# 29 small loads of different shapes between two weight loads at the end of a decode kernel

## Chip, core and metric

The kernel runs on one core of one Trainium2 chip. The metric is the device time of one execution in microseconds (us). The kernel before takes 1329.65 us (median of 3 runs, 1329.64 to 1329.71).

## What is computed

One decode step for a batch of two rows of 1024 numbers. A gate `g`, from the row and a weight vector, mixes two branches: `a` is multi-head attention over a cache, `b` a small MLP with two residual layers. Cut to what matters:

```python
B, Sq, D, H, Sk, Dh, F = 2, 1, 1024, 32, 16384, 128, 3584

def _A_ref(x, k_cache, v_cache, wq, wo):            # caches: (B, H, Sk, Dh), bf16
    q = (x @ wq).reshape(B, Sq, H, Dh).transpose(0, 2, 1, 3)
    scores = jnp.einsum("bhqd,bhkd->bhqk", q, k_cache) * (Dh ** -0.5)
    p = softmax(scores, axis=-1)
    o = jnp.einsum("bhqk,bhkd->bhqd", p, v_cache)
    return o.transpose(0, 2, 1, 3).reshape(B, Sq, H * Dh) @ wo

def _B_ref(x, w1, w2, w3, w4):
    h = gelu(layernorm(x) @ w1)
    hs = shifted(h) @ w2                            # parts of h moved along the sequence, which has length 1
    x1 = x + hs
    return x1 + gelu(layernorm(x1) @ w3) @ w4

g = sigmoid((x * gate_w).sum(-1, keepdims=True))
return g * a + (1 - g) * b
```

The caches are 2 x 32 x 16384 x 128 numbers of two bytes each for K and for V, 537 MB together. The rest, weights and inputs, is some 36 MB.

## The kernel before

**Tiles.** One large SBUF tile, `mem`, is cut into five cells of 16,384 numbers (32 KB) per partition; `region(cell, elements, offset)` names a part of it. A K or V block (two heads of one batch row, 128 partitions x 32,768 numbers, 8.4 MB, one transfer) fills two neighbouring cells: K goes to cells 0 and 1 for the first batch row and to 1 and 2 for the second (`K_CELL`), V to 3 and 4 (`V_CELL`), and the last V block to 0 and 1 (`V_LAST`).

**Loops.** Heads go in pairs (`HP` = 16 pairs, two batch rows each, so 32 units). A unit loads K, turns it in 128 x 2048 blocks on VectorE (line 435), forms the scores by matmuls on TensorE (line 441), takes the softmax (`softmax_a`, `softmax_b`), loads V and multiplies by it (`pv`, line 495), and scales the result (`pv_end`). `tc.For_i` runs over the pairs with `odd_unit` and `even_unit`; in the last round a `tc.If` block runs `last_unit`. The MLP's first layers run ahead of the loop.

**Order of transfers.** All large loads are issued by SyncE, from one queue and in program order (`load_k` line 113, `load_v` line 118, `load_weight` line 91); only w2 and the output go through ScalarE. `in_order()` ties each engine's instructions to the order of the program, so a transfer written between two others is issued between them. A load that would overwrite a cell waits at SyncE until the cell's readers are done, and all later issues wait behind it.

**The tail.** `last_unit` loads what the output needs, as listed in `TAIL`: piece 0 is wo (8.4 MB), 1 to 3 are w4 in 16, 9 and 3 of its 28 rows per partition, 4 to 6 the five rows of w1 that were left out at the start. Every row of a piece is 2 KB on each of 128 partitions. `load_tail(k)` (line 567) issues a piece and gives it a semaphore of its own, counted up by 16. Pieces 0 and 1 go to cells 3, 4 and 2 and are issued after `pv(0)`; the others go to cells 0 and 1, over the last V block, and stand after `pv(1, V_LAST)`. In `output()` TensorE waits for each piece in turn and runs its matmuls (`add_rows`, line 402): wo with the turned heads, w4 with `h2T`, then the rest of w1. `write_out()` runs after the last piece of w4 and stores the two rows; after the last piece of w1 a last gelu runs on ScalarE (line 663). At the very end GpSimd waits until the store has landed.

These lines of `output()` set the order in which the pieces are awaited:

```python
for k, (group, cell, at, src, r, n) in enumerate(TAIL):
    nc.tensor.wait_ge(tail_sems[k], 16)
```

Of the kernel before, what the change touches and what calls it, by code (L numbers as in the profile page):

```python
# [11 lines left out]
BF16 = mybir.dt.bfloat16  # L12
# [11 lines left out]
def kernel(  # L24
# [15 lines left out]
    nc = tc.nc  # L40
    P = nc.NUM_PARTITIONS
# [24 lines left out]
    const = ctx.enter_context(tc.tile_pool(name="const", bufs=1))  # L66
# [33 lines left out]
    rows = const.tile([B + 1, D], BF16, name="rows")  # L100
# [16 lines left out]
    def load_v(hp, b, cell=V_CELL):  # L117
        nc.sync.dma_start(out=region(cell, NJ * Dh), in_=cache_rows(A_v_cache, hp, b))
# [6 lines left out]
        out=ident_s[:], in0=ident_f[:], scalar1=-scale, scalar2=None, op0=ALU.mult  # L125
# [10 lines left out]
        out=mask4[:], in_=mask4[:], compare_op=ALU.is_ge, fill=0.0,  # L136
# [3 lines left out]
        out=mask4[:], in_=mask4[:], compare_op=ALU.is_ge, fill=0.0,  # L140
# [11 lines left out]
        out=lmat[:].rearrange("p (g h k) -> p g h k", h=2, k=4),  # L152
        in_=hm2[:].unsqueeze(1).unsqueeze(3).to_broadcast([P, P // 8, 2, 4]),
# [5 lines left out]
        out=lane[:],  # L159
        in_=ident_f[:].rearrange("p (c k) -> p k c", k=QP),  # L160
# [5 lines left out]
    for g in range(Q4):  # L166
        nc.vector.tensor_scalar(
            out=spread[:, g],
# [159 lines left out]
    for shift in (1, -1, 2, -2):  # L328
# [10 lines left out]
        out=x1_rows[:], in_=oacc[1][:, 0:G1], func=ACTF.Copy, scale=omg_row[:, 0:1]  # L339
# [21 lines left out]
    for k in range(2):  # L361
        wide = mlp.tile([P, 16, QP], FP32, tag="wide", name="wide")
        nc.scalar.activation(  # L363
            out=wide[:].rearrange("p (c e) i -> p c e i", e=2),
            in_=oacc[k][:].rearrange("p (c i e) -> p c e i", i=QP, e=2),
# [15 lines left out]
    for e in range(2):  # L381
        half = slice(e * HALF, (e + 1) * HALF)
        nc.vector.tensor_copy(
            out=qdu[half].rearrange("p u v -> p (u v)"),
            in_=qdps[half, e].rearrange("p k g n -> p (k g n)"),
# [27 lines left out]
    def begin_rows(into, saved):  # L413
        for g in range(Q4):
            nc.tensor.matmul(
                into[g][QP * g : QP * g + B, 0:G1],
                lhsT=ident_f[:, QP * g : QP * g + B],
                rhs=saved[:],
                start=True,
                stop=False,  # L420
                skip_group_check=True,
            )
# [29 lines left out]
    def score_first(hp, b):  # L452
        write_qw(hp, b)
        score_chunks(b, halves[1 - b], True, False)

    def score_second(b):
        score_chunks(b, halves[b], False, True)

    def softmax_a(b):
        S = S_tiles[b]  # L460
        st = ppool.tile([P, GT, QP], FP32, name="St")
        nc.vector.transpose(out=st[:].rearrange("p j r -> p (j r)"), in_=S[:])  # L462
        m = stat.tile([P, 1], FP32, name="m")
        nc.vector.tensor_reduce(out=m[:], in_=st[:, :, 0:NG], axis=AX.XY, op=ALU.max)  # L464
        Dm = ppool.tile([P, P], FP32, name="Dm")
        nc.scalar.activation(out=Dm[:], in_=ident_s[:], func=ACTF.Copy, scale=m[:, 0:1])  # L466
        st_tiles[b] = (st, Dm)

    def softmax_b(b):
        st, Dm = st_tiles.pop(b)  # L470
        R_ps = misc_psum([P, P])
        nc.tensor.matmul(R_ps[:], lhsT=ones_f[:], rhs=Dm[:], start=True, stop=True)  # L472
        nb = stat.tile([P, 1], FP32, name="nb")
        rs = stat.tile([P, 1], FP32, name="rs")
        parts = [slice(e * HALF, (e + 1) * HALF) for e in range(2)]
        for rows in parts:
            nc.vector.tensor_reduce(out=nb[rows], in_=R_ps[rows, rows], axis=AX.X, op=ALU.min)  # L477
        for e, rows in enumerate(parts):
            nc.scalar.activation(  # L479
                out=pts[b][rows, :, e, :].rearrange("p (m a) k -> p a k m", a=GT // 4),  # L480
                in_=st[rows, :, 0:NG].rearrange("p (a k) m -> p a k m", k=4),
                func=ACTF.Exp,
                bias=nb[rows],
                scale=scale,
                accum_out=rs[rows],
            )
        tot_ps = misc_psum([P, 1])
        nc.tensor.matmul(tot_ps[:], lhsT=lmat[:], rhs=rs[:], start=True, stop=True)  # L488
        nc.vector.reciprocal(out=rinvs[b][:], in_=tot_ps[:])  # L489

    def pv(b, cell=V_CELL):
        V = view(cell)
        for g in range(NJ // 4):
            q = g % Q4
            nc.tensor.matmul(  # L495
                oacc[b][QP * q : QP * q + 8, :],
                lhsT=pts[b][:, g].rearrange("p h k -> p (h k)"),
                rhs=V[:, 4 * g : 4 * g + 4, :].rearrange("p j d -> p (j d)"),
                start=(g < Q4),
                stop=(g >= NJ // 4 - Q4),  # L500
            )
# [4 lines left out]
    def pv_end(hp, b):  # L506
        osb = ppool.tile([P, 4 * Dh], FP32, name="osb")
        nc.scalar.activation(  # L508
            out=osb[:], in_=oacc[b][:], func=ACTF.Copy, scale=rinvs[b][:, 0:1]
        )  # L510
        ot = misc_psum([P, 2])
        for k in range(4):
            nc.tensor.matmul(  # L513
                ot[:], lhsT=osb[:, k * Dh : (k + 1) * Dh], rhs=lane[:, k : k + 5 : 4],
                start=(k == 0), stop=(k == 3),
            )
        nc.vector.tensor_scalar(  # L517
            out=o_all[:, b, bass.ds(2 * hp, 2)], in0=ot[:], scalar1=g_rep[:, b : b + 1],
            scalar2=None, op0=ALU.mult,
        )  # L520
# [5 lines left out]
    def turn_heads():  # L526
        apart = mlp.tile([P, B, H, Q4], BF16, name="apart")
        for b in range(B):
            nc.vector.tensor_tensor(
                out=apart[:, b],  # L530
                in0=o_all[:, b].unsqueeze(2).to_broadcast([P, H, Q4]),
                in1=mask4[:].unsqueeze(1).to_broadcast([P, H, Q4]),
                op=ALU.mult,
            )
        ps = misc_psum([P, B, QP])
        for b in range(B):
            nc.tensor.matmul(
                ps[:, b], lhsT=apart[:, b].rearrange("p h c -> p (h c)"), rhs=lane_b[:],
                start=True, stop=True,
            )  # L540
        t = mlp.tile([P, QP, B], BF16, name="o_turned")
        nc.vector.tensor_copy(out=t[:], in_=ps[:].rearrange("p b r -> p r b"))
        return t
# [17 lines left out]
    def tail_piece(k):  # L561
        group, cell, at, src, r, n = TAIL[k]
        return region(cell, n * D, at * D)

    def load_tail(k):
        group, cell, at, src, r, n = TAIL[k]
        dma = nc.sync.dma_start(out=tail_piece(k), in_=src[:, r * D : (r + n) * D])
        dma.then_inc(tail_sems[k], 16)
        tc.no_tile_sem_insts.add(dma.ins.name)
        tc.add_to_no_dep_group(group, dma.ins)  # L570


    end_mark = const.tile([1, 1], FP32, name="end_mark")
    stored = tc.alloc_semaphore("stored")
    out_row = mlp.tile([B, D], BF16, name="out_row")
# [51 lines left out]
    def last_unit(hp):  # L627
        V_LAST = 0
        score_first(hp, 1)
        load_v(hp, 1, V_LAST)  # L630
        score_second(1)
        softmax_a(1)
        pv(0)
        load_tail(0)
        load_tail(1)
        pv_end(hp, 0)
        softmax_b(1)
        pv(1, V_LAST)
        for k in range(2, len(TAIL)):
            load_tail(k)  # L640
        pv_end(hp, 1)

    def output():
        begin_rows(arows, x1_rows)
        o_turned = turn_heads()
        hidden = [oacc[0]] * Q4
        begin_rows(hidden, h_early)
        nc.scalar.activation(
            out=h_rows[0:1, 0:1], in_=o_turned[0:1, 0, 0:1], func=ACTF.Gelu_apprx_tanh
        )  # L650
        for k, (group, cell, at, src, r, n) in enumerate(TAIL):
            nc.tensor.wait_ge(tail_sems[k], 16)
            if src is wo_rows:
                add_rows(arows, o_turned, 0, tail_piece(k), False, group)
            elif src is w4_rows:
                mm = add_rows(arows, h2T, r, tail_piece(k), r + n == FC, group)
                if r + n == FC:
                    tc.declare_fence(mm.ins, group=group)
                    write_out()
            else:  # L660
                mm = add_rows(hidden, xn1T, r, tail_piece(k), r + n == KC, group)
                tc.declare_fence(mm.ins, group=group)
        nc.scalar.activation(out=h_rows[:], in_=oacc[0][:, 0:G1], func=ACTF.Gelu_apprx_tanh)  # L663
        mark = nc.gpsimd.memset(end_mark[:], 0.0)
        tc.declare_fence(mark.ins, group="stored")
        nc.gpsimd.wait_ge(stored, 16)

    def in_order():

# [59 lines left out]
```

## Time and profile before

| what | value |
|---|---|
| median of 3 runs | 1329.65 us |
| the profiled execution | 1329.7 us |
| its span, first to last instruction | 1327.7 us |
| TensorE clock granted, mean over the span | 0.782 |
| busy share: TensorE / VectorE / ScalarE / GpSimd | 57% / 49% / 10% / 1% |
| read from HBM | 572.53 MB, 431 GB/s over the span |
| SyncE: wo issued / its first matmul | 1272.94 / 1305.93 us |
| SyncE: last five pieces issued | 1288.85 to 1291.95 us |
| last instruction that computes (ScalarE, line 663) | ends 1326.87 us |

The engines are PE (TensorE matmul), PEld (TensorE weight load), DVE (VectorE), ACT (ScalarE), POOL (GpSimd) and SP (SyncE); a q behind the name (SPq) means the engine's sequencer, which issues transfers. L567 is line 567 of the kernel. The page gives the busy share of 40 equal slices of the span in tenths, with the transfer engines in the row DMA (mean over the core's 16 transfer engines). A transfer is cut into packets; a packet is what one transfer engine moves at a time. A row of a timeline has the start in us, the time from first to last of the merged instructions in us, engine, line, operation, tile and count, and in brackets the idle time before it with what ended it. A row of the stages has the stage, its length, the busy time (and count) of PE, PEld, DVE, ACT and POOL, the granted clock, the share of the transfer engines that was busy, and GB/s.

### The profile page before, as it was taken

The numbers are of one execution on the slowest core, as the hardware profiler recorded it, in microseconds if no ns is written. First come the engines' busy times: TensorE is split into PE (matmuls) and PEld (weight loads), VectorE is DVE, ScalarE is ACT, GpSimd is POOL, SyncE is SP. The second block draws the span as 40 slices with busy tenths as digits, with TensorE's granted clock in tenths as the row PEclk, the third lists the DMA queues.
The fourth block names the chain that finished last, engine by engine and source line by source line (L and its number), as shares of the span: only waits on it lengthen the run. The fifth ranks groups of instructions, "written<-read, shape, count | busy, mean of one in ns | idle before, by whom it ended". The sixth has DMA issues, their size and how long they took to land.

```text
span 1327.7 us, 12974 instructions
## 1 busy us (share of the span) xinstructions
PE 760.3 (57%) x4956; PEld 330.6 (25%) x4956; DVE 647.6 (49%) x507; ACT 132.5 (10%) x207; POOL 12.1 (1%) x48
## 2 busy tenths in 40 slices
PE   3465566655556665555666555566655556665554
PEld 1122222222222222222222222222222223222222
DVE  2554455554445555444555544455554445555420
ACT  0011110011111001111100111110011111101110
POOL 1000000000000000000000000000000000000000
PEclk9677888777788877778887777888777788877776
DMA  9999999999999999999999999999999999999998
GB/s 403 441 439 423 435 434 438 424 432 440 438 426 432 440 423 434 438 440 424 432 440 434 428 434 438 424 434 438 440 424 432 440 424 432 438 440 424 432 440 369
DMA packets 10820, 572.69 MB, mean 431 GB/s; under 512 B 1205, under 2 KB 1205, under 8 KB 1850
## 3 DMA queue, kind: packets, MB, share of 16 engines
q1 hardware_dynamic: 10662, 570.44, 99.4%
q10 hardware_dynamic: 148, 2.10, 0.4%
q8 instruction: 8, 0.13, 0.0%
q14 instruction: 2, 0.02, 0.0%
HBM read 572.53 MB, written 0.00 MB: 431 GB/s over the span
## 4 chain that ended last, share of the span: by engine, by line
DMA 61%; PE 11%; DVE 10%; issue 4%; ACT 0%; DVEq 0%; PEld 0%; SPq 0%; ACTq 0%
DMA mem<-in_A_k_cache_dram 59%; PE S L441 11%; DVE KT L435 10%; DMA mem<-in_B_w_dram 3%; PE oacc L495 0%; DVEq L435 0%; ACT pt L479 0%; PEld L495 0%; SPq L113 0%; PE misc L513 0%; PE oacc L402 0%; ACT osb L508 0%; PEld misc L488 0%; ACT h_rows L663 0%; PE misc L472 0%
## 5 line engine op out<-in xcount | busy, mean ns | idle before, releaser
L441 PE MATMUL S<-KT,qw 128*128 128x512 bf16 x2048 | 548.2, 418 | 363.2 <-DVE KT L435 362.8
L435 DVE STREAM_TRANSPOSE KT<-mem 128x2048 f32<-128x2048 f32 x256 | 570.7, 2282 | 270.9 <-DMA mem<-in_A_k_cache_dram 212.0
L441 PEld LDWEIGHTS <-qw 128*128 128x128 bf16 x2048 | 216.5, 106 | 686.8 <-issue 482.6
L495 PE MATMUL oacc<-mem,pt 128*8 128x512 bf16 x2048 | 118.2, 384 | 7.6 <-DMA mem<-in_A_v_cache_dram 7.6
L466 ACT ACTIVATE Dm<-ident_s,m 128x128 f32<-128x128 f32 x32 | 12.9, 402 | 978.5 <-PE oacc L495 941.4
L479 ACT ACTIVATE pt<-St,nb 64x256 bf16<-64x256 f32 x64 | 89.7, 1401 | 61.1 <-DVE nb L477 60.2
L517 DVE TENSOR_SCALAR o_all<-misc,g_rep 128x2 f32 (+1 forms) x32 | 7.0, 220 | 163.2 <-PE misc L513 163.2
L488 PE MATMUL misc<-rs,lmat 128*128 128x1 f32 x64 | 18.7, 362 | 107.9 <-ACT pt L479 61.3
L495 PEld LDWEIGHTS <-pt 128*8 128x8 bf16 x2048 | 47.3, 87 | 75.6 <-issue 23.8
L513 PE MATMUL misc<-lane,osb 128*128 128x2 f32 x256 | 33.4, 252 | 45.3 <-ACT osb L508 45.3
L489 DVE RECIPROCAL rinv<-misc 128x1 f32<-128x1 f32 x32 | 5.4, 169 | 108.5 <-PE misc L488 60.5
L462 DVE STREAM_TRANSPOSE St<-S 128x512 f32<-128x512 f32 x32 | 22.9, 717 | 66.4 <-PE L495 64.4
L513 PEld LDWEIGHTS misc<-lane,osb 128*128 128x128 f32 x256 | 31.1, 191 | 61.0 <-ACT osb L508 31.6
L488 PEld LDWEIGHTS misc<-rs,lmat 128*128 128x128 f32 x64 | 16.0, 311 | 114.8 <-ACT pt L479 65.3
L508 ACT ACTIVATE osb<-oacc,rinv 128x512 f32<-128x512 f32 x32 | 22.0, 687 | 88.3 <-PE oacc L495 88.3
L479 ACT ACTIVATION_READ_ACCUMULATOR pt<-St,nb 64x1 f32 x64 | 30.6, 477 | 0.0
L389 POOL TENSOR_TENSOR qw<-qdu,mask 128x16 bf16<-128x16 bf16 x32 | 7.3, 261 | 1161.6 <-PEq L688 1074.6
L477 DVE TENSOR_REDUCE nb<-misc 64x1 f32<-64x64 f32 x64 | 14.2, 222 | 7.0 <-PE misc L472 4.9
L472 PE MATMUL misc<-Dm,ones_f 128*128 128x128 f32 x64 | 16.6, 346 | 0.0
L464 DVE TENSOR_REDUCE m<-St 128x1 f32<-128x256 f32 x32 | 13.4, 420 | 1.1
L583 DVE CAST out_row<-arow 2x256 bf16<-2x256 f32 x1 | 0.4, 413 | 26.9 <-PE S L402 26.9
L217 DVE STREAM_TRANSPOSE turn<-wide 128x512 f32<-128x512 f32 (+2 forms) x4 | 3.0, 744 | 17.5 <-ACT wide L363 11.5
(104 smaller groups left out, 95.4 us busy)
## 6 DMA issues: line engine op xcount, KB each, us to landing
mem<-in_B_w_dram SPq DMA_DIRECT2D x1, 7168.0 KB, 31.6
mem<-in_B_w_dram SPq DMA_DIRECT2D x1, 4096.0 KB, 42.1
mem<-in_B_w_dram SPq DMA_DIRECT2D x1, 2304.0 KB, 32.2
mem<-in_B_w_dram ACTq DMA_DIRECT2D x1, 2048.0 KB, 11.8
mem<-in_B_w_dram SPq DMA_DIRECT2D x2, 768.0 KB, 21.1
mem<-in_B_w_dram SPq DMA_DIRECT2D x2, 512.0 KB, 33.9
mem<-in_A_k_cache_dram SPq DMA_DIRECT2D x32, 27.8
mem<-in_A_v_cache_dram SPq DMA_DIRECT2D x32, 32.4
```

The lines of the kernel that those rows point to most:

```text
L435: nc.vector.transpose(out=kt[:], in_=Kc.rearrange("p j d -> p (j d)").bitcast(FP32))
L441: nc.tensor.matmul(S, lhsT=qw[b][:, v, NG - 1 - m : NG - 1 - m + P], rhs=ktb[:, half * GT : (half + 1) * GT, w, :, e], start=(first and n ...
L462: nc.vector.transpose(out=st[:].rearrange("p j r -> p (j r)"), in_=S[:])
L464: nc.vector.tensor_reduce(out=m[:], in_=st[:, :, 0:NG], axis=AX.XY, op=ALU.max)
L466: nc.scalar.activation(out=Dm[:], in_=ident_s[:], func=ACTF.Copy, scale=m[:, 0:1])
L472: nc.tensor.matmul(R_ps[:], lhsT=ones_f[:], rhs=Dm[:], start=True, stop=True)
L477: nc.vector.tensor_reduce(out=nb[rows], in_=R_ps[rows, rows], axis=AX.X, op=ALU.min)
L479: nc.scalar.activation(out=pts[b][rows, :, e, :].rearrange("p (m a) k -> p a k m", a=GT // 4), in_=st[rows, :, 0:NG].rearrange("p (a k) m ...
L488: nc.tensor.matmul(tot_ps[:], lhsT=lmat[:], rhs=rs[:], start=True, stop=True)
L495: nc.tensor.matmul(oacc[b][QP * q : QP * q + 8, :], lhsT=pts[b][:, g].rearrange("p h k -> p (h k)"), rhs=V[:, 4 * g : 4 * g + 4, :].rearra ...
L508: nc.scalar.activation(out=osb[:], in_=oacc[b][:], func=ACTF.Copy, scale=rinvs[b][:, 0:1])
L513: nc.tensor.matmul(ot[:], lhsT=osb[:, k * Dh : (k + 1) * Dh], rhs=lane[:, k : k + 5 : 4], start=(k == 0), stop=(k == 3),)
```

## The change

A tile `marks` of 128 x 1280 numbers is added, which nothing reads, with a semaphore of its own. `load_marks()` issues 29 transfers from SyncE out of `wo` into it, one for each entry (first partition, rows, step, pieces) of `SHAPES`. Transfer number k takes 4 + 2k numbers of each row (8 to 120 bytes; the one with 16 pieces takes 3 numbers of each). The first 15 have 1 to 15 rows from partition 0; then come 16, 32 and 64 rows from partition 0, 64, 32 and 8 from partition 64, 8 and 16 rows with a step of 4 from partition 64, 16 with a step of 8, 96 rows, 4 rows from partition 96; and at last 3 rows in 4 pieces, 1 row in 16 and 8 rows in 2. A piece is a run of numbers 512 bytes after the one before. The call stands in `last_unit` between `load_tail(0)`, which loads wo, and `load_tail(1)`, the first piece of w4. The end of the program waits for the 29 transfers as well. In the order of each engine's instructions only SyncE's changes: 29 transfers between those of wo and w4. The result that is computed is the same.

```diff
@@ -570,6 +570,34 @@
         tc.add_to_no_dep_group(group, dma.ins)
 
 
+    marks = const.tile([P, 1280], BF16, name="marks")
+    marked = tc.alloc_semaphore("marked")
+    wo_flat = A_wo.rearrange("(p r) n -> p (r n)", p=P)
+    SHAPES = [(0, k, 1, 1) for k in range(1, 16)]
+    SHAPES += [
+        (0, 16, 1, 1), (0, 32, 1, 1), (0, 64, 1, 1), (64, 64, 1, 1), (64, 32, 1, 1), (64, 8, 1, 1),
+        (64, 8, 4, 1), (64, 16, 4, 1), (0, 16, 8, 1), (0, 96, 1, 1), (96, 4, 1, 1),
+        (0, 3, 1, 4), (0, 1, 1, 16), (0, 8, 1, 2),
+    ]
+
+    def load_marks():
+        at = 0
+        for k, (p, n, step, cuts) in enumerate(SHAPES):
+            wide = 3 if cuts == 16 else 4 + 2 * k
+            rows = slice(p, p + (n - 1) * step + 1, step)
+            dst = marks[rows, at : at + cuts * wide]
+            src = wo_flat[rows, 0 : cuts * 256]
+            if cuts > 1:
+                dst = dst.rearrange("p (c w) -> p c w", c=cuts)
+                src = src.rearrange("p (c w) -> p c w", c=cuts)[:, :, 0:wide]
+            else:
+                src = src[:, 0:wide]
+            dma = nc.sync.dma_start(out=dst, in_=src)
+            dma.then_inc(marked, 16)
+            tc.no_tile_sem_insts.add(dma.ins.name)
+            tc.add_to_no_dep_group("marked", dma.ins)
+            at += cuts * wide
+
     end_mark = const.tile([1, 1], FP32, name="end_mark")
@@ -632,6 +660,7 @@
         softmax_a(1)
         pv(0)
         load_tail(0)
+        load_marks()
         load_tail(1)
         pv_end(hp, 0)
         softmax_b(1)
@@ -663,7 +692,9 @@
         mark = nc.gpsimd.memset(end_mark[:], 0.0)
         tc.declare_fence(mark.ins, group="stored")
+        tc.declare_fence(mark.ins, group="marked")
         nc.gpsimd.wait_ge(stored, 16)
+        nc.gpsimd.wait_ge(marked, 16 * len(SHAPES))
```

## The prediction

> **What bounds the kernel now.** I read the page from the top: the slices, the queues, then the chain of waits.
>
> ```profile
> span 1327.7 us, 12974 instructions
> ...
> DMA  9999999999999999999999999999999999999998
> ...
> DMA packets 10820, 572.69 MB, mean 431 GB/s; under 512 B 1205, under 2 KB 1205, under 8 KB 1850
> ...
> q1 hardware_dynamic: 10662, 570.44, 99.4%
> ...
> DMA 61%; PE 11%; DVE 10%; issue 4%; ACT 0%; DVEq 0%; PEld 0%; SPq 0%; ACTq 0%
> ```
>
> The transfer engines are busy in every slice but the last, nearly all of it on q1, the queue that SyncE fills; the chain goes through transfers for 61%. The kernel is bound by the stream of bytes. So a step costs what it adds to the stream, plus any hole that it tears in it.
>
> Next the last stretch: SyncE's timeline around the change, then the weight loads of the tail matmuls, each of which starts when its piece has landed.
>
> ```profile
> 1258.12 0.34 SPq L118 DMA_DIRECT2D mem<-in_A_v_cache_dram  x1
> 1272.94 0.34 SPq L567 DMA_DIRECT2D mem<-in_A_wo_dram  x1
> 1273.39 0.36 SPq L567 DMA_DIRECT2D mem<-in_B_w_dram  x1
> 1288.85 3.10 SPq L567 DMA_DIRECT2D mem<-in_B_w_dram  x5
> ```
> ```profile
> 1305.90 6.01 PEld L402 LDWEIGHTS <-o_turned 128*2 128x2 bf16 x128 [9.23 <-issue]
> 1315.55 2.87 PEld L402 LDWEIGHTS <-h2T 128*2 128x2 bf16 x64 [3.63 <-DMA mem<-in_B_w_dram]
> 1321.05 1.13 PEld L402 LDWEIGHTS <-h2T 128*2 128x2 bf16 x36 [2.63 <-DMA mem<-in_B_w_dram]
> 1322.92 0.31 PEld L402 LDWEIGHTS <-h2T 128*2 128x2 bf16 x12 [0.74 <-DMA mem<-in_B_w_dram]
> 1324.21 0.10 PEld L402 LDWEIGHTS <-xn1T 128*2 128x2 bf16 x8 [0.98 <-DMA mem<-in_B_w_dram]
> 1325.43 0.10 PEld L402 LDWEIGHTS <-xn1T 128*2 128x2 bf16 x8 [1.12 <-DMA mem<-in_B_w_dram]
> 1326.06 0.09 PEld L402 LDWEIGHTS <-xn1T 128*2 128x2 bf16 x4 [0.53 <-DMA mem<-in_B_w_dram]
> ```
>
> SyncE issues wo at 1272.94 and the first piece of w4 at 1273.39; the rest goes out from 1288.85 on, once the last V load and its matmuls are done. The queue is deep: wo is needed at 1305.90, 33 us after its issue, the first w4 piece at 1315.55, 42 us after. TensorE waits for every later piece, and from 1326.06 to the end only 1.7 us of fixed work follow. What the queue takes longer between wo and w4, the end takes longer.
>
> Last, how the stream ends, by stages of the tail (the last two columns are the busy share of the 16 engines and GB/s):
>
> ```profile
> 1321.00:1322.90 1.90, 1.64 (x36) 0.92 (x36) 0.00 (x0) 0.00 (x0) 0.00 (x0) 0.65 1.00 401
> 1322.90:1324.20 1.30, 0.81 (x12) 0.24 (x12) 0.41 (x1) 0.38 (x2) 0.00 (x0) 0.50 0.92 364
> 1324.20:1325.40 1.20, 0.60 (x8) 0.10 (x8) 0.42 (x1) 0.37 (x1) 0.00 (x0) 0.50 0.52 203
> 1325.40:1326.00 0.60, 0.57 (x8) 0.10 (x8) 0.00 (x0) 0.00 (x0) 0.00 (x0) 0.50 0.07 21
> ```
>
> The 16 engines do not stop together: in 1324.2 to 1325.4 only about half are busy, while TensorE still waits for the slower ones. An engine that ends early has up to about 1 us of room.
>
> **What the change adds: packets.** It removes nothing. Its 29 transfers name 520 rows or pieces of rows (120 in the first fifteen; 16+32+64+64+32+8+8+16+16+96+4, which is 356; 12+16+16 in the last three) and 39,856 bytes. How they fall on engines follows from a count: q1 holds 74 loads of 128 rows (w1 early, wq, w3, 32 K, 32 V, 7 of the tail) and the three rows of x and the gate. 74 x 128 + 3 is 9475; 74 x 16 + 3 is 1187; the sum is the 10662 of the page. So a row is one packet, a 128-row load ends in 16 completion packets, and x with two rows and the gate with one row together in three. I read this as: a transfer of n rows below 16 uses n engines, one row each; 32, 64 and 96 rows use 16 engines with 2, 4 and 6 each. The trace does not name engines; I assume that the lists start at the same one. That engine then gets one packet in each of the first 16 transfers, then 2+4+4+2+1+1+1+1+6+1, then 4+1+2: 46 data packets and 29 completions. The engine with least is only in the transfers of 16 rows and their multiples, and in the 16 pieces: 22 and 9.
>
> The Trainium skill (DMA: Bandwidth & Descriptors, "Why a DMA increments its semaphore by 16 and not by 1") says that the largest number up to 16 that divides both slowest dimensions is used, and the lowest-numbered engines. The trace agrees as far as the three small completions go; by that rule the busiest engine has the same 46 and 29.
>
> **The price of a packet.** No row shows a transfer of 8 to 120 bytes in a running stream. The landings give lines to extend: pieces of 9, 3, 2, 2 and 1 rows of w landed 5.50 (1321.05-1315.55), 1.87, 1.29, 1.22 and 0.63 us apart. At eight packets for each engine, 9 rows make 0.69 us per packet of 18 KB and one row 0.079 us per packet of 2 KB: 38 and 39 ns per KB, so a packet's own overhead is near 10 ns at most, and a whole transfer's fixed part lies between 0 and 0.06 us.
> - Lower end: by bytes alone, 39,856 B at 431 GB/s, 0.1 us. A gain has one small source: 16 KB instruction fetches share the engines (8 packets, 0.13 MB on q8; 0.6 us each at the tail's rate), and the new code could put one elsewhere: -0.6 us.
> - Upper end: each small packet at the 0.079 us of a 2 KB one and each transfer at 0.06: 46 x 0.079 + 29 x 0.06 = 5.4 us.
> - Taken: the line is nearer to the small packet than the 2 KB row is, since that row's time is nearly all bytes. I take 0.025 us per data packet, twice the overhead and a little for the bytes, and 0.02 per completion: 46 x 0.025 + 29 x 0.02 = 1.15 + 0.58 = 1.73 us on the busiest engine, all on the path if it is a slow one. If it is an early one, 0.7 of that shows, or the least-loaded engine's 22 x 0.025 + 9 x 0.02 = 0.73 decides. The trace does not say which; I take the full 1.73.
>
> The Trainium skill (same page, "Specifications") puts 512 B as the least for line rate and says that below it the engine reads, modifies and writes. All 520 pieces are below. Nothing here shows the penalty; counted as twice the taken price, the sum would be 2.9 us.
>
> **SyncE's issues.** 29 instructions go ahead of the first w4 piece and of the wait for the last V. What an issue takes is seen where SyncE waits for nothing, at the start of its timeline; the third and the second are small transfers:
>
> ```profile
> 0.80 0.38 SPq L98 DMA_DIRECT2D mem<-in_B_w_dram  x1
> 1.25 0.33 SPq L101 DMA_DIRECT2D rows<-in_A_x_dram  x1
> 1.63 0.22 SPq L102 DMA_DIRECT2D rows<-in_gate_w_dram  x1
> 1.89 0.36 SPq L91 DMA_DIRECT2D mem<-in_A_wq_dram  x1
> ```
>
> They follow each other by 0.26 to 0.45 us, wo and w4 by 0.45, so 29 x 0.45 = 13.0 us: w4 goes out at 1286.4 instead of 1273.4. It is covered by V, which lands at 1286.47, and by wo, until 1305.3 at the engines. The five later pieces are held until 1288.85 anyway, so they do not move. With the 0.53 us of the output's issue and a gap of 0.1, it is 18.3 us: w4 at 1291.7, the five done at 1295; still covered. The cover is gone only above (1305.3 - 1.0 - 1273.4) / 29 = 1.07 us each, 1.0 being the time from the first issue (0.80) to the first busy engines (in 1.5 to 2.0 us). Cost: nothing.
>
> **The end.** GpSimd waits for the 29 completions too, behind the wait for the stored output; nothing is queued behind it but the end of the program. They are ahead of w4 in the queue and so some 10 us early. Cost: nothing. No instruction of the other engines is added.
>
> **Sum.** 1.73 us on a span of 1327.7, with the 2.0 us that the profiled execution (1329.7) has around it. That is 0.05 above the median of the runs shown, 1329.65; so 1331.4.
>
> **The rivals.**
> 1. *Small rows are dear.* The engines take the same 46 packets, but at 0.045 us or more each (read-modify-write, or reads that no longer overlap). From 0.045 on the sum passes 2.66 us; at the upper end it is 5.4: 1332.3 to 1335. For it: no row below 2 KB in the stream. Against it: the line above.
> 2. *The queue is full and the stream gets a hole*; this ends on the slower side. SyncE can run only so many transfers ahead. The trace shows at most seven (wo and six pieces, at 1291.95), each issued in 0.33 to 0.37 us; after the change it is over thirty. If 16 fit, wo and 15 small ones sit there until 1305.3; the 15 drain at once, and the engines starve while SyncE issues 14 more and w4: 15 x 0.45 + 1.0 = 7.8 us, 1337.4. At 24 it is 7 x 0.45 + 1.0 = 4.2 us, 1333.8; at 8, 11.4 us, 1341. It decides below about 30 places. For it: nothing in the trace goes deeper than seven. Against it: no issue there is slowed.
> 3. *One transfer after the other.* If a small transfer kept its engines until it landed, at the 1.0 us from issue to first data each, 29 us: 1358.7. Against it: the pieces of 0.63 and 1.22 us land back to back. The Trainium skill (same page, "Anatomy of one DMA — SWDGE (gpsimd) path") has a fixed 2.0 us per transfer, mostly its receipt; paid in series that would be an estimated 58 us. The five pieces show no such term.
> 4. *It is hidden, or a fetch moves off the slowest engine*: 1329.0 to 1329.9.
>
> **How the numbers follow.** The measurement tells about 0.2% (2.66 us) from no change. Forecast, 1329.7 to 1332.3: 0.43. Rival 1: 0.21. Rival 2: 0.27. Rival 3: 0.02. Rival 4: 0.07, half of it a gain, nearly all of that under 0.2%. Slower by over 0.2% are rivals 1 to 3, 0.50; within, 0.48; faster, 0.02. The range holds 1329.6 to 1338.0, from rival 4 to a queue of 16 places; outside are a shallower queue, rival 3 and a gain. The forecast's own range is 1329.7 to 1332.3.
>
> **What would show it.** On q1, 520 more data packets and about 310 completions (by the split above), near 11,490. Right: wo needed at 1305.9 as before, w4's first piece 1 to 2.6 us later than 1315.55, the gaps after it unchanged, and the engines' share at 1 across 1305. Rival 1: the same, but the shift above 2.7 us. Rival 2: issues of L595 far above 0.4 us, or running until past 1305, and a slice with the engines idle. I am wrong if the shift arises ahead of wo, or if w4's gaps grow.

## The result and the profile after

The changed kernel takes 1333.43 us (median of 9 runs, 1332.97 to 1333.72) against 1329.67 (9 runs beside them): 3.76 us more, ratio 1.0028, 95% interval 1.0018 to 1.0038. The profiled execution has a span of 1331.3 us, 3.5 more than before.

First the page of the changed kernel: span, packets, the queue of SyncE, and the chain by engine.

```profile
span 1331.3 us, 13004 instructions
...
DMA packets 11634, 572.72 MB, mean 430 GB/s; under 512 B 2020, under 2 KB 2020, under 8 KB 2665
...
q1 hardware_dynamic: 11477, 570.48, 99.3%
...
DMA 60%; DVE 10%; PE 10%; issue 4%; SPq 2%; DVEq 0%; ACT 0%
```

q1 has 815 packets more: the 520 data packets and 295 completions. (A completion is the last packet of a transfer on an engine, 4 bytes in the trace; with it the engine counts up the transfer's semaphore.) The split by rows gives 295 exactly (the "about 310" of the prediction was an error of addition). New in the chain is SPq, SyncE's issuing, with 2%. Its timeline and the chain around it:

```profile
1272.96 0.34 SPq L567 DMA_DIRECT2D mem<-in_A_wo_dram  x1
1273.35 28.74 SPq L595 DMA_DIRECT2D marks<-in_A_wo_dram  x29
1302.23 2.91 SPq L567 DMA_DIRECT2D mem<-in_B_w_dram  x6
```
```profile
1284.53 1.81 SPq L595
1286.34 0.04 issue
1286.38 14.59 SPq L595
```

The 29 issues took 28.7 us instead of the 13 that were forecast, mainly because one of them, the transfer of 3 rows in 4 pieces, was held for 14.59 us. The first piece of w4 went out at 1302.23 instead of 1273.39. Now the weight loads of the tail matmuls, from the last part of wo on:

```profile
1314.62 3.47 PEld L402 LDWEIGHTS <-o_turned 128*2 128x2 bf16 x71 [3.21 <-issue]
1319.20 1.50 PEld L402 LDWEIGHTS <-h2T 128*2 128x2 bf16 x57 [1.11 <-DMA mem<-in_B_w_dram]
...
1324.72 1.43 PEld L402 LDWEIGHTS <-h2T 128*2 128x2 bf16 x36 [3.52 <-DMA mem<-in_B_w_dram]
1326.60 0.30 PEld L402 LDWEIGHTS <-h2T 128*2 128x2 bf16 x12 [0.46 <-DMA mem<-in_B_w_dram]
...
1329.68 0.09 PEld L402 LDWEIGHTS <-xn1T 128*2 128x2 bf16 x4 [0.53 <-DMA mem<-in_B_w_dram]
```

The first piece of w4 is there at 1319.20, 3.65 us later than the 1315.55 of before; all later pieces are late by the same (1324.72 against 1321.05, 1329.68 against 1326.06). wo itself lands within 0.2 us of before (last engine 1305.97 against 1305.79). So nearly all of the loss arises between the end of wo and the landing of that piece. The stages show where the bytes were missing (last columns: share of the engines, GB/s; a packet's time and bytes are counted where it starts). The changed kernel:

```profile
1303.00:1305.50 2.50, 0.00 (x0) 0.00 (x0) 0.00 (x0) 0.00 (x0) 0.00 (x0) 0.50 1.46 186
1305.50:1306.00 0.50, 0.00 (x0) 0.00 (x0) 0.00 (x0) 0.00 (x0) 0.00 (x0) 0.50 1.04 268
1306.00:1308.00 2.00, 1.35 (x10) 0.36 (x14) 0.62 (x3) 1.28 (x1) 0.09 (x1) 0.50 0.37 131
1308.00:1310.00 2.00, 2.00 (x36) 1.16 (x32) 0.10 (x1) 0.20 (x1) 0.00 (x0) 0.50 0.91 344
```

and the kernel before:

```profile
1303.00:1305.50 2.50, 0.00 (x0) 0.00 (x0) 0.00 (x0) 0.00 (x0) 0.00 (x0) 0.50 0.76 328
1305.50:1306.00 0.50, 0.07 (x4) 0.10 (x8) 0.00 (x0) 0.00 (x0) 0.00 (x0) 0.50 0.61 262
1306.00:1308.00 2.00, 2.00 (x40) 1.28 (x43) 0.00 (x0) 0.00 (x0) 0.00 (x0) 0.50 1.06 459
1308.00:1310.00 2.00, 2.00 (x48) 1.32 (x40) 0.00 (x0) 0.00 (x0) 0.00 (x0) 0.50 0.99 426
```

In the seven microseconds from 1303 to 1310 the changed kernel started packets of 186 x 2.5 + 268 x 0.5 + 131 x 2 + 344 x 2, some 1.55 MB, the one before 2.72 MB. The 1.17 MB that are missing are 2.7 us at 430 GB/s. That is the mean over the engines: by the semaphore records the sixteen parts of the first w4 piece, one per engine, land 2.7 us later on average, the last of them 3.66 us (1319.16 against 1315.50), and the piece is there with the last. The shares over 1 are packets that start in the stage and are recorded as running beyond it.

This picture has two readings. Either SyncE, held by a full queue, brought w4 too late and the engines ran dry; that is what the chain names. Or the small transfers kept the engines, although most of their packet records are 9 to 13 ns long (a few near the end up to 0.36 us) and the last of them starts at 1305.69. The experiments decide between them.

### The profile page after: what moved, and what is told of

Read it like the earlier page. It is cut to its first block, busy times and chain, and to the rows that moved or that the text cites. A ratio compares the mean times of both kernels' runs of the same rounds, so it can differ in the third digit from the quotient of the medians.

```text
span 1331.3 us, 13004 instructions
## 1 busy us (share of the span) xinstructions
PE 760.1 (57%) x4956; PEld 331.2 (25%) x4956; DVE 648.0 (49%) x507; ACT 132.5 (10%) x207; POOL 12.0 (1%) x48
## 4 chain that ended last, share of the span: by engine, by line
DMA 60%; DVE 10%; PE 10%; issue 4%; SPq 2%; DVEq 0%; ACT 0%
DMA mem<-in_A_k_cache_dram 59%; DVE KT L435 10%; PE S L441 10%; SPq L595 2%; DMA mem<-in_B_w_dram 2%; PE oacc L495 0%; DVEq L435 0%; SPq L567 0%; SPq L113 0%; ACT h_rows L692 0%; PE oacc L402 0%; DVEq L462 0%
## 5 line engine op out<-in xcount | busy, mean ns | idle before, releaser
L472 PEld LDWEIGHTS misc<-Dm,ones_f 128*128 128x128 f32 x64 | 11.2, 219 | 0.4 <-issue 0.4
```

## The experiments

"Before" in each is the time of the unchanged kernel beside it: 1329.80 for the first four, 1329.77 for the next four, 1329.90 for the last four. The 95% intervals are about 1.3 us wide to each side, so sizes that lie closer together than that are told apart by the traces, where they are, and not by the times. A lead is the time by which an engine ends wo ahead of the last one.

**1. The first 15 transfers alone**

```diff
+    SHAPES = SHAPES[:15]
     def load_marks():
```

> Only the first 15 of the 29 transfers (1 to 15 rows; 120 rows, on the busiest engine 15 data packets and 15 completions of 46 and 29). Full queue: SyncE was held only from the 26th transfer on, so here no issue is held, w4 goes out near 1278.6 us, there is no hole and the time is 1329.7 to 1330.3. Packets' own time: the 3.76 us fall with the packets of the busiest engine, 30 of 75, so about +1.5 us, 1331.2. Shape: as the full queue, since the 3 rows in 4 pieces are left out.

Measured 1330.88 us, +1.08, ratio 1.0009 (0.9999 to 1.0018). No small issue was held and w4 went out at 1278.94, yet its first piece stood at 1316.75, 1.2 us late. The late issue does not explain this; the packets' own time fits better (+1.5). By its interval the time alone does not quite exclude no change; the piece that lands 1.2 us late is the stronger sign.

**2. Without the transfer whose issue was held**

```diff
-        (0, 3, 1, 4), (0, 1, 1, 16), (0, 8, 1, 2),
+        (0, 1, 1, 16), (0, 8, 1, 2),
```

> All but the transfer of 3 rows in 4 pieces, whose issue took 14.59 us. Full queue: the next transfers are held in its place, w4 goes out at 1299 us or later and the time is 1332.5 to 1333.5. Shape: nothing is held for more than the 1.8 us before it, w4 goes out near 1287.6 and the time is 1329.8 to 1330.5. Packets' own time: 4 data packets and 1 completion fewer of 75, 1333.2.

Measured 1333.41, +3.61, ratio 1.0027 (1.0017 to 1.0037). The next transfer was held in its place for 14.43 us. The hold is not a matter of the shape.

**3. That transfer alone**

```diff
+    SHAPES = [(0, 3, 1, 4)]
     def load_marks():
```

> Only the transfer of 3 rows in 4 pieces. Full queue: its issue takes 0.3 to 0.6 us. Shape: its issue takes over 10 us, w4 goes out near 1288, still covered by wo. Both: time 1329.6 to 1329.9. Packets' own time: 5 of 75 packets, +0.25 us.

Measured 1329.92, +0.12, ratio 1.0001 (0.9991 to 1.0010): no difference. Its issue took 0.31 us.

**4. The transfers behind all pieces**

```diff
@@ last_unit
-        load_marks()
         load_tail(1)
@@ output
     def output():
+        load_marks()
         begin_rows(arows, x1_rows)
```

> All 29 transfers, but issued by SyncE after the loop, behind all seven pieces, so that nothing waits behind them at SyncE but the end of the program. Full queue: the issues are held again, but no piece is late; the first matmul on w4 stands at 1315.5 as before and the time is 1329.7 to 1331 (what is over 1329.7 is the small transfers that land last). Packets' own time: the engines have the same work in all, so 1333 or more.

Measured 1333.68, +3.88, ratio 1.0029 (1.0017 to 1.0040). In the order that was built the first four transfers went out ahead of the loop (at 75 us) and the other 25 after it, behind all pieces; the last issue ended at 1323.8 us. The tail's last pieces, the stages of the end, and nothing after them:

```profile
1325.58 0.10 PEld L402 LDWEIGHTS <-xn1T 128*2 128x2 bf16 x8 [1.18 <-DMA mem<-in_B_w_dram]
1326.31 0.09 PEld L402 LDWEIGHTS <-xn1T 128*2 128x2 bf16 x4 [0.63 <-DMA mem<-in_B_w_dram]
1326.75 0.38 ACT L692 ACTIVATE h_rows<-oacc 128x256 bf16<-128x256 f32 x1 [2.03 <-PE oacc L402]
```
```profile
1325.00:1326.00 1.00, 0.42 (x8) 0.10 (x8) 0.00 (x0) 0.00 (x0) 0.00 (x0) 0.50 0.67 128
1326.00:1327.00 1.00, 0.56 (x8) 0.09 (x4) 0.00 (x0) 0.25 (x1) 0.00 (x0) 0.50 0.00 0
1327.00:1328.00 1.00, 0.00 (x0) 0.00 (x0) 0.00 (x0) 0.13 (x1) 0.00 (x0) 0.50 0.00 0
1328.00:1329.00 1.00, 0.00 (x0) 0.00 (x0) 0.00 (x0) 0.00 (x0) 0.00 (x0) 0.50 0.00 0
```

Every piece is as early as before to 0.25 us (1326.31 against 1326.06), the last gelu ends at 1327.1, the program's last packet is recorded at 1325.96, and still the span ends at 1331.6. The semaphore records tell why: the completions of the small transfers come in until 1330.52, 6.7 us after the last issue. With no late issue in the way of any piece, the price is the same. The reading by the late issue, as I had written it, falls; what the small transfers cost, they cost on the engines, and not in their packets but in their completions. The last completions of 29 transfers of one row each (experiment 5) show the beat, in us:

```
1308.13  1308.32  1308.51  1308.70  1308.90  1309.08  1309.26  1309.44
```

They are about 0.18 us apart; all 29 come at this beat, from 1304.30 on. The new theory: on an engine a small transfer must be completed before the next one's completion goes out, 0.18 us each, and what stands behind them waits. The change then costs 0.18 us x completions on an engine, less what that engine was ahead. How far each is ahead can be read from where its first small packet starts, since transfer n of the first 15 is the first on its n-th engine and its row has a length of its own. In the changed kernel (start in us, bytes):

```
1303.562 8     first engine, 29 completions
1305.061 28    sixth engine, 22 completions
1305.405 52    twelfth engine, the last to finish wo
```

So the first engine is 1.84 us ahead, the sixth 0.34. (The fourth, with 25 completions and 0.85 us, comes out like the sixth by this working.) The next experiments price rivals of this theory.

**5. 29 transfers of one row**

```diff
+    SHAPES = [(0, 1, 1, 1)] * 29
     def load_marks():
```

> 29 transfers of one row each (29 data packets, 29 completions, by the split all on one engine, which finishes wo about 1.8 us ahead of the slowest). A completion takes its engine some 0.2 us, one after the other: 29 x 0.2 - 1.8 = +4.0 us, 1333.7. Rival, completions queue at the one semaphore they all count up (295 in some 6 us in the changed kernel, 0.02 us each): 29 x 0.02, nothing, 1329.8. Rival, each small data packet costs 0.13 us (5.8 us over 46): 29 x 0.13 - 1.8 = +2.0, 1331.7. Late issue alone: none is held, 1329.8.

Measured 1332.56, +2.79, ratio 1.0021 (1.0011 to 1.0030). A queue at the shared semaphore and the late issue are out: they gave nothing. Their 29 issues took 8.6 us, w4 went out at 1282.21. The size lies between the two per-engine theories (4.0 with 0.2 us, 3.4 with the 0.18 that the beat shows; 2.0 by data packets).

The semaphore of the first w4 piece shows whom the small transfers hit. Fifteen of its sixteen parts land between 1313.69 and 1315.53, as before (1313.64 to 1315.50); one lands at 1318.36. In the packet records, too, one packet of that piece is drawn out: it has 32 KB, for which the kernel before takes 1.21 us, and runs from 1303.99 to 1309.00. w4 had been issued 22 us earlier. So the engine with the 29 transfers is held, and no other.

**6. 29 transfers of 16 rows**

```diff
+    SHAPES = [(16 * (k % 8), 16, 1, 1) for k in range(29)]
     def load_marks():
```

> 29 transfers of 16 rows (464 data packets and 464 completions, one of each per transfer on every engine, so the engines that finish wo last have them too). A completion takes its engine 0.2 us: 29 x 0.2 with no room, +5.8 us, 1335.5. Completions queue at the one semaphore: 464 x 0.02 = 9.3 us less up to 1.8, 1337 or more. Each data packet costs 0.13 us: +3.8, 1333.5. Late issue alone: as much or as little as with one row each.

Measured 1334.98, +5.21, ratio 1.0038 (1.0024 to 1.0052). 29 x 0.18 is 5.2: now the engines that finish last have the completions as well, and nothing is covered. 16 times the completions of experiment 5 do not cost 16 times as much.

**7. 8 transfers of 16 rows with 3 KB each**

```diff
-    marks = const.tile([P, 1280], BF16, name="marks")
+    marks = const.tile([P, 1536], BF16, name="marks")
+    SHAPES = [(16 * k, 16, 1, 1) for k in range(8)]
-            wide = 3 if cuts == 16 else 4 + 2 * k
+            wide, at = 1536, 0
-            src = wo_flat[rows, 0 : cuts * 256]
+            src = wo_flat[rows, 0:1536]
-            at += cuts * wide
```

> 8 transfers of 16 rows with 3 KB in each row (0.12 us of data for each engine, at 0.079 us per 2 KB). If the completion's 0.2 us runs beside the transfer's data: 8 x 0.2 = +1.6 us, 1331.4. If it comes on top: 8 x 0.32 = +2.6 us, 1332.3. If small rows alone were the cost: 8 x 0.12 = +1.0, 1330.7.

Measured 1332.52, +2.75, ratio 1.0021 (1.0011 to 1.0031): 0.34 us per transfer, nearest to the completion on top of 0.12 us of data. (The interval reaches from 1.5 to 4.1 us and takes in +1.6 as well; all ten runs, 1332.28 to 1332.73, lie nearer to 1332.3.)

**8. 12 transfers of 64 rows**

```diff
+    SHAPES = [(64 * (k % 2), 64, 1, 1) for k in range(12)]
     def load_marks():
```

> 12 transfers of 64 rows of 8 to 52 bytes: on every engine 48 data packets, more than the 46 of the busiest engine in the changed kernel, and 12 completions. Per completion 0.2 us: +2.4 us, 1332.2. Per data packet 0.13 us: +6.2 us, 1336.

Measured 1331.55, +1.78, ratio 1.0013 (1.0003 to 1.0022): 0.15 us per transfer, with 48 data packets on every engine. The +6.2 us by data packets are far outside. Data packets of 8 to 52 bytes cost next to nothing.

**9. 22 transfers of six rows**

```diff
+    SHAPES = [(0, 6, 1, 1)] * 22
     def load_marks():
```

> 22 transfers of 6 rows: by the split the first six engines get 22 completions each, and the sixth finishes wo only 0.3 us ahead of the slowest (1305.06 against 1305.40 in the changed kernel); in the changed kernel it has 22 completions too. If a completion takes its engine 0.18 us and the engine that is then last sets the end: 22 x 0.18 - 0.3 = +3.6 us, 1333.4, more than 29 transfers of one row (+2.8) and as much as the change. If only the number of transfers counted: 22/29 of +2.8, 1331.9.

Measured 1333.32, +3.42, ratio 1.0026 (1.0016 to 1.0035). Seven transfers fewer than in experiment 5 cost 0.6 us more. The two intervals overlap, but the trace shows the reason: six parts of the first w4 piece land late, from 1316.95 to 1318.93, the other ten by 1315.44, and among the six is an engine with little room. It is also within 0.4 us of the whole change, in which that engine has the same 22.

**10. The transfers ahead of the loop, from ScalarE's queue**

```diff
     softmax_b(0)
+    load_marks()
@@ load_marks
-            dma = nc.sync.dma_start(out=dst, in_=src)
+            dma = nc.scalar.dma_start(out=dst, in_=src)
@@ last_unit
-        load_marks()
```

> All 29 transfers issued by ScalarE ahead of the loop, in its own queue beside the K and V loads. If a completion holds only its own queue, the engines move K and V in between and the packets alone are paid: 1329.7 to 1330.3. If it holds the whole engine: 22 to 29 completions of 0.18 us as after wo, +2.5 to +3.8, 1332.3 to 1333.6. In both, ScalarE issues for some 13 us in a stretch in which it has 30 us without work.

Measured 1330.37, +0.47, ratio 1.0004 (0.9994 to 1.0014), not told apart from nothing and below the +2.5 of a held engine. The 29 were issued from 78.9 to 92.1 us and were complete by 241 us, between the packets of K and V.

**11. The same from SyncE's queue**

```diff
     softmax_b(0)
+    load_marks()
@@ last_unit
-        load_marks()
```

> The same 29 transfers at the same place, issued by SyncE in the queue of the loads. If a completion holds its queue: +2.5 to +3.8 us, 1332.3 to 1333.6, as in the tail (the stream is full there too), and more if the next K load goes out late behind a held issue. If the place in the tail were what costs: 1329.7 to 1330.3.

Measured 1333.93, +4.03, ratio 1.0030 (1.0018 to 1.0041). This run does not say what it was made for: again only four transfers were ordered ahead of the loop and 25 behind all pieces, so that it repeats experiment 4 (completions until 1330.45). Whether experiment 10 owes its price to the other queue or to the place stays open.

**12. w4 late, without small transfers**

```diff
-        ("tail", V_CELL, 0, wo_rows, 0, QP),
+        ("tail", V_CELL, 0, wo_rows, 0, 26),
+        ("tail", V_CELL, 26, wo_rows, 26, 6),
@@ last_unit
         load_tail(0)
         load_tail(1)
+        nc.sync.wait_ge(tail_sems[0], 16)
+        load_tail(2)
@@ last_unit, output
-        for k in range(2, len(TAIL)):
+        for k in range(3, len(TAIL)):
-                add_rows(arows, o_turned, 0, tail_piece(k), False, group)
+                add_rows(arows, o_turned, r, tail_piece(k), False, group)
```

> No small transfers. wo is cut into 26 and 6 rows, and SyncE waits for the first part (about 1302.1 us) before it issues the first piece of w4, so that w4 goes out at the time of the changed kernel (1302.23). If the late issue of w4 tears a hole: +2 us or more, up to the 3.7 of the change. If the completions alone are the cost: 1329.7 to 1330.3.

Measured 1330.16, +0.26, ratio 1.0002 (0.9993 to 1.0012). Its SyncE, its first w4 matmuls, and its stages over the end of wo:

```profile
1302.21 2.80 SPq L568 DMA_DIRECT2D mem<-in_B_w_dram  x6
```
```profile
1315.79 1.50 PEld L402 LDWEIGHTS <-h2T 128*2 128x2 bf16 x57 [0.19 <-DMA mem<-in_B_w_dram]
```
```profile
1303.00:1305.50 2.50, 0.00 (x0) 0.00 (x0) 0.00 (x0) 0.00 (x0) 0.00 (x0) 0.50 1.27 487
...
1306.00:1308.00 2.00, 1.07 (x6) 0.24 (x6) 0.49 (x2) 1.11 (x1) 0.09 (x1) 0.50 1.06 459
```

w4 goes out at 1302.21, as late as in the changed kernel (1302.23), and its first piece is there at 1315.79, 0.24 us after that of before. From 1306 to 1308 the engines move 459 GB/s, not 131. The first w4 packet of each engine, 1.21 us long in the kernel before, takes 1.2 to 2.1 us here and 1.7 to 4.3 us in the changed kernel, where these packets start between 1303.84 and 1305.70: there the engines have w4 and are held. An issue about 1 us ahead of the first engine's end of wo is early enough. The 28.7 us of issues that the chain runs through cost nothing by themselves.

**The sizes together.** Shift worked out as 0.18 us x completions, less the engine's lead, for the engine that is worst off:

| kernel | worst engine | worked out, us | measured, us |
|---|---|---|---|
| the change | sixth, 22 x 0.18 - 0.34 | 3.6 | 3.76 |
| 1: first 15 | sixth, 10 x 0.18 - 0.34 | 1.5 | 1.08 |
| 2: without 3 rows in 4 pieces | sixth, 22 | 3.6 | 3.61 |
| 3: that one alone | first, 1 x 0.18 - 1.84 | none | 0.12 |
| 5: 29 of one row | first, 29 x 0.18 - 1.84 | 3.4 | 2.79 |
| 6: 29 of 16 rows | all, 29 x 0.18 | 5.2 | 5.21 |
| 7: 8 of 16 rows, 3 KB | all, 8 x (0.18 + 0.12) | 2.4 | 2.75 |
| 8: 12 of 64 rows | all, 12 x 0.18 | 2.2 | 1.78 |
| 9: 22 of six rows | sixth, 22 x 0.18 - 0.34 | 3.6 | 3.42 |

Experiments 4, 10 and 11 have the transfers elsewhere in the stream and are left out. The rest, from 0.6 us below to 0.35 above, is not settled. That the w4 packets behind are partly moved in the meantime would explain the smaller ones. Experiment 5 points that way: the drawn-out packet takes 5.0 us and not 29 x 0.18 + 1.21, and it ends 0.44 us ahead of the last small completion (1309.00 against 1309.44). No run was made to test it. Nor can times tell the completion from another fixed step that a transfer has on each engine; for the completion speaks that the counts come in at this beat, after the last packet record.

## Why the prediction was right and where it was wrong

- **What bounds the kernel, and how a delay passes on**: right. What the queue took longer between wo and w4, 3.65 us, the end took longer, with the gaps of the later pieces unchanged.
- **How the packets fall on engines**: right. A row a packet, n rows on n engines, 520 and 295 in the count. The rule of the Trainium skill (DMA: Bandwidth & Descriptors, "Why a DMA increments its semaphore by 16 and not by 1"), the lowest-numbered engines, fits too as far as the trace tells, which does not number engines: 22 transfers of six rows make six parts of w4 late, 29 of one row make one late.
- **The price of a packet, 46 x 0.025 = 1.15 us**: too high. With 48 data packets on every engine experiment 8 stays below what its 12 completions alone would cost. The Trainium skill gives no size with its rule for pieces below 512 B (same page, "Specifications"); the doubled price that I put on it, 2.9 us in all, is not seen in experiment 8.
- **The price of a completion, 29 x 0.02 = 0.58 us**: this is the step that failed, by a factor of nine. It is 0.18 us, 5.2 for 29. I took it from the landings of five pieces of w, whose fixed part is 0 to 0.06 us. But these keep an engine busy with data for 0.6 us or more; a 2 KB row in each of 16 partitions would have been a nearer row, and the trace has none. Experiment 7 has 0.12 us of data and pays in full; between 0.12 and 0.6 us the price goes away. Where, and whether it is the data that cover it, is open.
- **The room of an early engine**: right in kind. I gave it about 1 us; the first engine has 1.84 in the changed kernel, and the sixth, with 0.34 and 22 completions, sets the end instead. I had taken the engine with most packets to be a slow one; it is among the early ones.
- **SyncE's issues cost nothing**: right, for another reason than the one given. The issues were not 13 us but 28.7, since one was held, and w4 was not early by 19 us but by 1. Experiment 12 shows that this is enough.
- **The end**: right for the change; the completions were in at 1310.2, about 20 us ahead.
- **The forecast's own range, 1329.7 to 1332.3**: missed by 1.1 us; the wide range held. That was luck as far as the mechanism goes: its upper part was there for rivals 1 and 2, and what happened is neither. *Rival 1* gave the right time for the wrong reason: it is not the rows that are dear. The hold of *rival 2* came, at some 75 packets, and had no price, since it ended before wo did. I had let 15 of the transfers fit and SyncE stand still until 1305.3. *Rival 3* had the right mechanism, one completion after the other, with a price of 1.0 us instead of 0.18; I ruled it out by the same five pieces. The Trainium skill's 2.0 us per transfer (same page, "Anatomy of one DMA — SWDGE (gpsimd) path") is for a single transfer by itself on that other path; one behind the other, the small transfers here took 0.18 us each, an eleventh.
- **What would show it**: wo was not needed "at 1305.9 as before". SyncE left the loop late, so TensorE began with wo at 1308.15. That was covered, as its wo matmuls end at 1318.1 and w4 lands at 1319.2. The signs that I listed for rival 2, an issue far above 0.4 us (14.59) and a slice with idle engines (share 0.37 from 1306 to 1308), both came true although late issue was not the cause. They do not tell an engine that has nothing to do from one that is held; the landings by engine do.

## What to carry to other kernels

Ahead of other loads in the same queue a small transfer costs its completion, here some 0.18 us on each engine that it touches, and not its bytes or rows (whether another queue avoids this is open after experiments 10 and 11): count transfers per engine, merge them, and watch the engine that is last anyway. A price read from large pieces can hide such a term: pieces with 0.6 us of data per engine showed at most 0.06 us of it. And a chain that names a held issue names a wait, not a cost; whether the cover was really used up has to be tried, as by issuing late on purpose.

## What the runs showed of the hardware

- The packet record of a completion does not show when the completion is in: in the changed kernel the last small packet starts at 1305.69, and the last completion is counted at 1310.20; in experiment 4 these are 1325.96 and 1330.52.
- SyncE was held when a transfer engine had some 75 packets outstanding, counted with all of wo's. In the changed kernel the first engine had wo's 9 and 65 small ones when the next 5 were held. In experiment 5 it had 9 + 58 + 9, and the next w4 piece was held for 12 us:

```profile
1288.88 14.03 SPq L567 DMA_DIRECT2D mem<-in_B_w_dram  x5
```

  The count is not sharp: in experiment 2 a request that would have made it 76 was held, in experiments 8 and 9 requests to 78 and 80 were let through after 5.2 and 3.3 us. The long holds of experiments 1, 2, 5 and 6 and of the change all ended between 1300.9 and 1301.2, some 2.4 us before the first engine ended wo; those of experiments 8 and 9 ended at 1302.8 and 1302.4. What ends them is open.
- Without a hold, an issue took 0.22 to 0.42 us for 1 to 16 neighbouring rows and 0.55 to 0.60 us for 64 or 96 rows.
- The 16 engines end wo (8.4 MB) over some 1.9 us. In the three runs where it could be read (the change and experiments 1 and 2) the same ones are last: the 6th and the 12th to 15th, with the 4th next.
